# Another order list, pair evictions and four copies moved to GpSimd in an attention-and-maxout kernel

## The chip, the cores and the metric

The kernel runs on one core of one Trainium2 chip. Its time is the device time of one launch in microseconds (us), the median of several runs. A trace of one further execution, taken by the hardware profiler, shows every instruction on the five engines: TensorE (PE, with its weight loads PEld), VectorE (DVE), ScalarE (ACT), GpSimd (POOL) and SyncE (SP, which only issues transfers here).

## What is computed

x has 4 batches of 12544 rows with 128 channels; there are 32 inducing rows; w1 and w2 are 128 x 1024, w_out is 1024 x 128.

```python
def mab(q, kv):
    s = scale * (q @ kv.transpose(0, 2, 1))
    a = softmax(s)
    return a @ kv
h = mab(I, x)                 # 32 rows pool over all of x, per batch
y = mab(x, h)                 # each row of x attends to those 32 rows
h1, h2 = y @ w1, y @ w2
out = np.maximum(h1, h2) @ w_out
```

## The kernel before

The kernel uses max(h1, h2) = h1 + relu(h2 - h1). Both products are linear in h, so for each batch it works out two small matrices: hwd = h (w2 - w1), 32 x 1024, and m1 = h w1 w_out, 32 x 128. With e = exp of the scores of a row against the 32 rows of h, the output row is (relu(e hwd) w_out + e m1), divided by the sum of e.

Per batch there is a pooling part (letters in the order list: x = DMA transposes of x, c = scores and exp, t = DMA transpose of the exponentials, a = accumulation, r = the rest, e, h, w, m = the small matrices) and the main part:

- *stage* (s, L712/L725): scores of a block of up to 16 chunks of 128 rows, four quarters on the four 32-column strips of PE; ACT writes e into an SBUF tile (six of them).
- *phase* (p, L1205): up to four jobs, one per quarter, on the four 32-row strips of PE at once. Each job writes 512 columns of e hwd into one of the eight PSUM banks. In the same stretch the e m1 part of the group that is about to end may run on the fourth strip.
- *eviction of a job* (relu_out, L1107 on DVE, L1110 on ACT): relu from PSUM into an SBUF tile. The number behind the first dot of a phase word is a mask that says which jobs go to DVE. A second number, if given, is a mask of jobs to hold: a held job's eviction waits for the next phase, and if that brings the following job of the same quarter, both banks are evicted in one instruction; any word that isn't a phase lets go of held jobs one by one. The list before has no such second numbers.
- *finals* (plain numbers, L989): so many full 128 x 128 matmuls, relu tile times w_out, added up in one PSUM bank per group of up to four chunks.
- *eviction of a group* (evict_group): multiply by the reciprocal of the sums, on DVE (L1024) or, where the string EVICT has a 1, on ACT (L1031, one instruction per chunk); then SP stores it. There are six output slots.
- *turn_e2* (g, L767 to L780): DMA transpose of e, then halving additions and a reciprocal on POOL. A block without it gets its sums from PE (L819) and DVE (L829).

PE has three kinds of tiling in this kernel: full (finals, transposes, small matrices), row strips (phases) and column strips (stages, pooling). All instructions are issued in the order in which the Python code records them. That order is the string ORDER, one word after another. While recording, the class Clock keeps a rough account of when each engine and bank is free; from that account come the choice of the PSUM bank of each step, the number of filler matmuls (dummies, L619, and keep_busy, L945), and nothing else that is issued.

At the head, w2 - w1 is made on DVE and POOL (difference, L623), H is the step that makes the second half of hwd for batch 0, V transposes w1 on PE (L641) and copies it to SBUF as w1T (L646 DVE, L649 ACT), and W multiplies it with w_out (L662).

small_m1 (L596 to L613) makes m1 on PE and evicts it; for the last batch it also writes the same four 32-row pieces into m1bd, a block-diagonal copy that the last block's full-size matmuls read (linear_full, L963).

The line that assigns an eviction to an engine within a phase:

```python
relu_out(q, blk, [before[1], unit], before[2], ready, vector >> k & 1)
```

## Time and profile before

| | |
|---|---|
| median of 3 runs | 314.69 us (314.38 to 314.78) |
| the profiled execution's own time | 314.68 us |
| its span | 312.9 us |
| granted TensorE clock | 0.998 |
| finals L989, relus | 3104 matmuls |
| relu evictions on ACT (L1110) | 468, mean 620 ns |
| relu evictions on DVE (L1107) | 308, mean 683 ns |
| group evictions on DVE (L1024, 128x512) | 68 and 21 |

The span is what the trace covers, from its first to its last instruction; the execution's time has 1.8 us around it. In rows by group, the columns are: line, engine, operation, what is written and read, shapes and count; then busy us and mean ns of one; then the engine's idle time ahead of such instructions and who ended it. In the chain in order of time a row is: start, us, what ran. In rows of stages: the stretch, its length, then busy us and instructions of each engine, the granted clock, the DMA share, GB/s.

### The profile page before, as it was taken

What the parts mean: (1) busy time and instruction counts of PE and PEld (TensorE: products, weight loads), DVE (VectorE), ACT (ScalarE), POOL (GpSimd) and SP (SyncE); (2) the same over time, 40 slices, a digit from 0 to 9 for tenths busy, and PEclk for the clock granted to TensorE, in tenths of its full rate; (3) what the DMA queues carried; (4) which work ended last, traced back from release to release, by engine and by line L of the source; (5) the groups of instructions that cost most, each with busy time, mean ns of one, the idle gap of its engine ahead of it and who ended that gap; (6) DMA issues with size and microseconds to landing.
All of it is one profiled execution on the core that took longest, in us unless ns stands there. A gap on an engine that the chain in (4) does not pass through costs nothing.

```text
span 312.9 us, 12567 instructions
## 1 busy us (share of the span) xinstructions
PE 306.0 (98%) x5316; PEld 239.4 (77%) x5316; DVE 273.1 (87%) x485; ACT 280.7 (90%) x581; POOL 122.6 (39%) x183
## 2 busy tenths in 40 slices
PE   6999999999999999999999999999999999999996
PEld 2875777777877777778877887778778877788885
DVE  2458999999889999988999998999999899989894
ACT  3668999999989989999999999989999899998875
POOL 7374007910530006677500565139205743288000
PEclk9999999999999999999999999999999999999999
DMA  7999999999399999989699999993422522342223
GB/s 206 208 255 203 218 214 192 167 231 232 107 204 244 256 212 202 212 199 218 136 241 256 185 241 200 194 229 114 131 86 103 153 102 87 118 130 103 103 88 136
DMA packets 80793, 55.69 MB, mean 178 GB/s; under 512 B 62272, under 2 KB 65632, under 8 KB 80736
## 3 DMA queue, kind: packets, MB, share of 16 engines
q1 hardware_dynamic: 74768, 41.19, 56.5%
q0 software_dynamic: 5968, 13.70, 22.6%
q8 instruction: 41, 0.67, 0.9%
q14 instruction: 16, 0.13, 0.1%
HBM read 27.28 MB, written 25.69 MB: 169 GB/s over the span
## 4 chain that ended last, share of the span: by engine, by line
PE 94%; DMA 3%; DVE 1%; issue 1%; POOL 0%; ACT 0%; POOLq 0%
PE psall L989 61%; PE psall L1205 23%; DMA xn<-in_x_dram 3%; PE psall L712 2%; PE psall L458 1%; PE psall L399 1%; PE psall L309 1%; PE psall L371 1%; PE psall L325 1%; DVE relus L1107 1%; PE psall L571 1%; PE psall L504 0%; PE psall L362 0%; DVE hwd L575 0%; PE psall L819 0%
## 5 line engine op out<-in xcount | busy, mean ns | idle before, releaser
L1110 ACT ACTIVATE relus<-psall 128x512 f16<-128x512 f32 x468 | 239.2, 620 | 15.4 <-PE psall L1205 14.4
L1107 DVE TENSOR_SCALAR relus<-psall 128x512 f16<-128x512 f32 x308 | 195.5, 683 | 16.6 <-PE psall L1205 15.7
L989 PE MATMUL psall<-woutp,relus 128*128 128x128 f16 x3104 | 203.7, 220 | 0.0
L989 PEld LDWEIGHTS <-relus 128*128 128x128 f16 x3104 | 174.9, 98 | 33.1 <-issue 27.3
L1205 PE MATMUL psall<-e,hwd 32*128 32x512 f16 (+2 forms) x840 | 81.1, 362 | 0.0
L776 POOL TENSOR_TENSOR half<-ed 128x256 f32<-128x256 f16 (+2 forms) x22 | 13.4, 611 | 145.5 <-DMA ed<-e 145.5
L780 POOL TENSOR_TENSOR rd<-den,minus 128x16 f32<-128x16 f32 (+2 forms) x22 | 57.8, 2628 | 1.7
L1024 DVE TENSOR_TENSOR osbs<-psall,rd 128x512 f32<-128x512 f32 (+1 forms) x80 | 50.9, 637 | 4.3 <-PE psall L1205 1.3
L1205 PEld LDWEIGHTS <-hwd 32*128 32x128 f16 x880 | 27.9, 91 | 11.7 <-issue 2.3
L1205 PE MATMUL psall<-m,e 32*128 32x128 f16 x372 | 36.6, 216 | 0.0
L1205 PEld LDWEIGHTS <-e 32*128 32x128 f16 x372 | 22.2, 92 | 9.6 <-issue 2.0
L776 POOL TENSOR_TENSOR half<-half 128x32 f32<-128x32 f32 (+4 forms) x66 | 21.4, 324 | 5.2
L228 POOL DMA_DIRECT2D xn<-in_x_dram x32 | 17.8, 569 | 5.7 <-DMA xn<-in_x_dram 4.3
L1024 DVE TENSOR_TENSOR osbs<-psall,rp 128x512 f32<-128x512 f32 (+3 forms) x24 | 15.6, 649 | 0.5 <-PE psall L1205 0.4
L313 DVE COPY xT<-psall 128x512 f16<-128x512 f16 (+3 forms) x12 | 5.7, 485 | 8.6 <-PE psall L309 8.4
L413 ACT ACTIVATE eu<-psall 128x512 f16<-128x512 f32 x18 | 10.8, 612 | 0.3 <-PE psall L399 0.2
L725 ACT ACTIVATE e<-psall 128x512 f16<-128x512 f32 (+2 forms) x21 | 10.9, 574 | 0.1
L316 ACT COPY xT<-psall 128x768 f16<-128x768 f16 (+3 forms) x10 | 5.8, 576 | 4.6 <-PE psall L309 4.5
L309 PE MATMUL psall<-identity,xn 128*128 128x128 f16 x98 | 7.5, 219 | 1.5 <-DMA xn<-in_x_dram 1.0
L712 PE MATMUL psall<-xT,hT 128*32 128x512 f16 (+3 forms) x110 | 8.4, 362 | 0.0
L309 PEld LDWEIGHTS <-xn 128*128 128x128 f16 x98 | 5.5, 97 | 3.1 <-DMA xn<-in_x_dram 1.4
L399 PE MATMUL psall<-xT,inducingT 128*32 128x512 f16 x72 | 6.4, 381 | 0.0
(114 smaller groups left out, 129.8 us busy)
## 6 DMA issues: line engine op xcount, KB each, us to landing
out_dram<-osbs SPq DMA_DIRECT2D x90, 256.0 KB, 2.9
xn<-in_x_dram POOLq DMA_DIRECT2D x24, 448.0 KB, 9.9
out_dram<-osbs SPq DMA_DIRECT2D x10, 128.0 KB, 4.3
relus<-in_moe_w_dram POOLq DMA_DIRECT2D x4, 256.0 KB, 5.7
xn<-in_x_dram POOLq DMA_DIRECT2D x4, 224.0 KB, 10.3
xT<-xn SPq DMA_TRANSPOSE x33, 4.3
relus<-in_x_dram SPq DMA_DIRECT2D x1, 512.0 KB, 4.0
relus<-in_x_dram SPq DMA_DIRECT2D x1, 384.0 KB, 4.4
```

Of the source, the lines that this page charges most:

```text
L228: nc.gpsimd.dma_start(out=xn_at[b, i][:, 0:n, :], in_=xr[b, :, k0 : k0 + n, :])
L309: nc.tensor.transpose(ps[:, j, :], xn[:, g + j, :], identity16)
L413: nc.scalar.activation(out=eu, in_=ps, func=AF.Exp, scale=scale, accum_out=st[b]["es"][:, u : u + 1])
L712: nc.tensor.matmul(out=ps[32 * q : 32 * (q + 1), 128 * t : 128 * (t + n)], lhsT=hq, rhs=xT[:, c : c + n, :], start=True, stop=True, tile_p ...
L725: nc.scalar.activation(out=blk.e2[:, 0 : 128 * wd], in_=ps[:, 0 : 128 * wd], func=AF.Exp, scale=st[0]["rs"] if blk.b == 0 else scale,)
L776: nc.gpsimd.tensor_tensor(out=dst, in0=cur[:, :, 0:n], in1=cur[:, :, n : 2 * n], op=ALU.add)
L780: nc.gpsimd.tensor_tensor(out=rp[:, 0:wd, :].rearrange("p t q -> p (t q)"), in0=den[:, 0 : 4 * wd], in1=minus1[:, 0 : 4 * wd], op=ALU.pow,)
L989: nc.tensor.matmul(out=g.ps[lo:hi, 128 * c : 128 * (c + 1)], lhsT=relu[:, lo:hi], rhs=woutp[:, jb, :], start=not g.started, stop=(state["m ...
L1024: nc.vector.tensor_mul(osb[:, 0:m, :], g.ps[:, 0 : m * C].rearrange("p (s c) -> p s c", s=m), g.blk.rp[:, t0 : t0 + m, q : q + 1].broadcas ...
L1107: nc.vector.tensor_scalar(out=dst, in0=src, scalar1=0.0, scalar2=None, op0=ALU.max)
L1110: nc.scalar.activation(out=dst, in_=src, func=AF.Relu)
L1205: nc.tensor.matmul(**seq.pop(0))
```

## The change

Five things change. The constants of Clock: a pair of finals, the switch from row strips to full, the times of two POOL steps. In small_m1 the pieces of m1bd are no longer written by DVE from PSUM but copied by GpSimd from m1. The string ORDER is another list; it also uses hold masks (56 of them), and it puts the transposes x, the turns g, the stages and the finals at other places. EVICT has five ones at other places instead of four, and the last group goes to DVE. The head's order becomes "s p4.12.2 p1.0.1 x1.0 p1.1.1 H1 s V W p2.2 x1.1 p4.8" in place of "s p4.9 s p2.2 H1 V W p2.2 p4.2".

```diff
--- before.py
+++ after.py
@@ -21,11 +21,11 @@
 class Clock:
 
 
-    PAIR = 0.0563
+    PAIR = 0.0559
     COLS = 0.0566
     SWITCH = {
         "full": {"row": 0.095, "col": 0.095},
-        "row": {"full": 0.082, "col": 0.088},
+        "row": {"full": 0.0985, "col": 0.088},
         "col": {"full": 0.1, "row": 0.094},
     }
     STEP = 0.0035
@@ -600,15 +600,17 @@
             end = ck.run(0.06)
             m1 = smp.tile([128, C], F16, name=f"m1_{b}", tag="m1")
             bd = {B - 1: [0, 1, 2, 3]}.get(b, [])
-            outs = [(m1bd[32 * q : 32 * (q + 1), q, :], slice(32 * q, 32 * (q + 1))) for q in bd]
-            for o, r in outs + [(m1, slice(0, 128))]:
-                if b == 0:
-                    nc.vector.tensor_scalar(
-                        out=o, in0=ps[r, 0:128], scalar1=st[0]["rw"][r, :], scalar2=None, op0=ALU.mult
-                    )
-                else:
-                    nc.vector.tensor_copy(out=o, in_=ps[r, 0:128])
-                ck.bank[bi] = ck.on_dve(end, 0.28)
+            if b == 0:
+                nc.vector.tensor_scalar(
+                    out=m1, in0=ps[:, 0:128], scalar1=st[0]["rw"], scalar2=None, op0=ALU.mult
+                )
+            else:
+                nc.vector.tensor_copy(out=m1, in_=ps[:, 0:128])
+            ck.bank[bi] = ck.on_dve(end, 0.28)
+            for q in bd:
+                r = slice(32 * q, 32 * (q + 1))
+                nc.gpsimd.tensor_copy(out=m1bd[r, q, :], in_=m1[r, :])
+                ck.on_pool(ck.bank[bi], 0.3)
             st[b]["m1"] = m1
             st[b]["m1r"] = ck.bank[bi]
 
@@ -630,7 +632,7 @@
                 ck.on_dve(20.4, 0.33)
             else:
                 nc.gpsimd.tensor_copy(out=w1h[:, sl], in_=w1f[:, sl])
-                w_of["cast"] = ck.on_pool(0.0, 0.8)
+                w_of["cast"] = ck.on_pool(0.0, 0.62)
 
         def weights_2():
             turned = []
@@ -885,7 +887,8 @@
         difference(nc.gpsimd, 256, 512, 21.0, 0.64)
         load_x(1, 1)
         load_x(1, 2)
-        difference(nc.gpsimd, 512, J, 22.9, 1.25)
+        ck.pool = 22.98
+        difference(nc.gpsimd, 512, J, 22.9, 1.28)
         cast_w1(1)
         for i in range(3, 7):
             load_x(1, i)
@@ -1227,33 +1230,34 @@
 
         state["stage"] = 1
         ORDER = """
-        s p4.9 s p2.2 H1 V W p2.2 p4.2 14 m0 p3.1 4 p3.2 4 p3.3 15 p4.2 6 x1.0 2 p3.6 15 p4.8 13 p4.5 14
-        p3.1 x1.1 10 p1 p4.6 14 p4.1 20 p4.5 p2.2 16 s x1.2 s p3.5 15 p4.1 g3 18 g4 p3.4 p2.1 x1.3 11
-        x1.4 p4.5 14 p4.1 14 p3.3 10 p4.5 s c1.0 18 p2.1 g5 p3.1 x1.5 x1.6 6 x1.7 6 p4.9 11 x1.8 12 p3.6
-        p3.4 17 s c1.1 p3.4 12 x1.9 3 p4.12 3 x1.10 4 p3.2 11 p4.1 21 p4.2 p2.1 21 p4.6 t1.1 12 p1 p4.5
-        14 c1.2 c1.3 p4.10 23 p3.2 t1.3 p3.2 23 p4.3 18 p2.1 p4.8 28 p4.12 p2 23 g6 p4.5 a1.1 c1.4 a1.3
-        c1.5 p3.4 11 r1 t1.5 14 p4.8 p3.2 31 p2.1 p4.4 9 a1.5 p4.8 5 e1 17 h1 5 p4.3 p3.1 21 w1 6 s s
-        p4.10 25 p3.1 p3.4 33 p4.3 p3.1 24 s s p3.4 18 p2.2 p4.2 11 m1 13 p3.4 4 p4.12 21 p1 p3.2 15 p2.2
-        p4.2 18 p4.5 15 p1.1 p4.2 x2.0 x2.1 14 x2.2 3 p4.5 6 x2.3 13 x2.4 p4.4 p2.1 14 g9 9 x2.5 p3.6 p2
-        13 p4.9 21 p2.2 p4.2 31 x2.6 x2.7 p3.5 p4.1 26 x2.8 g10 c2.0 s p4.12 21 p2.1 p4.8 23 p4.3 10 p3.3
-        c2.1 s c2.2 13 p3.1 7 t2.1 1 p4.3 8 x2.9 2 g11 x2.10 g12 4 p4.3 16 p4.8 13 p4.12 15 p3.2 15 c2.3
-        p3.4 p3.1 28 p3.4 p3.4 22 p4.5 13 s t2.3 c2.4 a2.1 c2.5 p3.1 p3.1 21 g13 7 p2.1 t2.5 p4.2 28 p2.1
-        p4.10 6 r2 22 p3.6 p3 24 p4.1 a2.3 a2.5 p3.2 5 p4.6 14 p4.1 e2 24 p4.3 p3 12 h2 19 p4.1 p2.1 18
-        p4.10 10 p3.4 12 w2 6 p4.14 s s s 23 p2.2 p4.1 24 p3.6 s p3.2 14 p4.8 8 m2 6 p4.4 23 p3.1 p2.2 12
-        g17 2 x3.0 g15 p4.8 21 p2.1 x3.1 x3.2 p4.8 29 p3.1 x3.3 p4.10 24 p3.4 11 p4.9 x3.4 13 p4.4 16
-        p4.10 21 p3.1 p3.2 11 x3.5 x3.6 g1 g16 10 p4.1 x3.7 21 p2.1 p4.1 31 p3.2 p4.3 29 p4.5 10 x3.8
-        p3.5 s s c3.0 c3.1 13 p4.12 18 p3.3 p2 2 t3.1 9 x3.9 x3.10 3 p4.1 18 p3.5 p3 27 p4.9 p2.1 19 s
-        c3.2 c3.3 a3.1 p4.10 p2.1 19 g19 t3.3 g18 p4.9 21 p3.1 p3.1 20 p4.5 r3 21 p3.2 p3.2 31 p4.14 p3
-        27 p4.12 a3.3 c3.4 c3.5 11 p3.3 p3 8 t3.5 23 g20 p4.8 p3.3 31 p2.1 p4.8 23 p4.6 a3.5 p1 p3.4 10
-        p4.1 2 g7 1 e3 10 g14 7 h3 6 p4.3 p3.2 14 w3 3 m3 5 s s s 11 g21 p1 p4.4 21 p4.10 12 p1 p4.6 15
-        p4.8 19 p2.3 p4.2 28 g23 p2.2 p4.2 19 p3.4 3 g22 19 p3.2 p4.6 39 p3.1 p3.2 31 p4.10 p3.2 31 p4.3
-        p2 22 p4.5 11 p3.1 8 p4.1 17 p4.10 14 p3.6 s s s 11 p4.2 8 p3.5 14 g24 p4.1 16 p4.9 12 p4.1 p1.1
-        g8 23 p4.14 p2 15 s p4.1 21 p4.8 p2.1 30 g27 p4.2 p3.5 20 g26 p4.1 18 g25 3 p2.2 p4.1 31 p3.3
-        p4.4 28 p4.12 p1 17 p4.3 18 p2.2 p4.8 31 p3.4 p4.6 1 g2 30 p2.2 p4.8 31 p3.1 p4.5 32 p4.5 p2 30
-        p4.10 p2 24 p4.8 p2.1 32 p3.6 p3.1 23 p2.3 p4.1 36 p2.1 p3.1 24 p4.1 p4.7 56
+        s p4.12.2 p1.0.1 x1.0 p1.1.1 H1 s V W p2.2 x1.1 p4.8 11 m0 4 p3.1.3 4 p3.1 5 p3.5 13 p4.4 11 x1.2
+        p3.4 10 p4.10 13 p4.3 7 x1.3 p3 17 p3.3.1 p2.2.1 11 p4.2 24 p2.1.1 p4.2 22 p3.5 s s 5 p4.10 22
+        p3.5 p2 x1.4 13 p4.6 4 x1.5 10 p4.8.1 g3 13 x1.6 x1.7 g1 p3.5 11 p4.5 c1.0 s 1 x1.8 18 p2.2
+        p3.1.4 11 p4.9 23 p3.5 p3 22 p3.5 x1.9 c1.1 s 11 p4.6 7 p3.2.1 10 p4.1 g4 5 g5 16 p3.5.5 p3.2 21
+        p4.12 10 x1.10 t1.1 p1 p4.6 15 p4.12 c1.2 c1.3 21 p3.3 p3 3 t1.3 19 p4.9 19 p4.15.12 p2 30 p4.1
+        g6 p2.2 22 p4.11 3 c1.4 c1.5 a1.1 a1.3 p3.4 8 r1 t1.5 18 p4.13.15 p3.4 33 p2.2 p4.2 9 a1.5 p4.2 4
+        e1 17 h1 5 p4.10 p3.1 20 w1 6 s s p4.3 24 p3.2.7 p3.2 32 p3.3.2 p4.5 23 s s p3.4 16 p4.1.15 p2.1
+        28 p3.1 p4.1.1 22 m1 p1.1 p3 18 p2.2 p4.1 13 g10 8 p4.12 12 p1 p4.5 8 x2.0 x2.1 5 x2.2 p4.3 21
+        p2.0.1 p4.10 19 x2.3 x2.4 g9 7 p3.2.5 p2.1.1 11 p4.5 x2.5 21 p2.0.2 x2.6 p4.6 x2.7 31 p4.12 p3.2
+        26 s c2.0 p4.6 21 g11 p2.1 p4.2 23 p4.6 10 p3.6 x2.8 c2.1 x2.9 c2.2 s 16 p3.1 3 t2.1 2 x2.10
+        p4.12 14 p4.4 14 p4.3 14 p4.5 g12 14 p3.4 c2.3 15 p2.3.2 p4.2 28 p3.1 p3.4 23 p4.9 t2.3 11 s c2.4
+        a2.1 c2.5 p3.1 p3.4 28 p2.1 t2.5 g13 p4.1 28 p4.4 p2.1 28 r2 2 p3.2 p3.4 24 g8 p4.8 a2.3 a2.5
+        p3.4 5 p4.5 9 e2 4 p4.2 23 h2 4 p4.8 p3.1 31 p4.12.2 p2 21 p4.10 11 p3.1 w2 12 p4.9 s s s 22 p2.2
+        p4.4.1 26 p3.1 s p3.6 14 p4.4 4 m2 14 p4.3 19 p2 p3.6 11 p4.1 g15 2 g16 19 p3.5.1 p3.0.5 x3.0 30
+        x3.1 p3.2 p4.9 x3.2 9 x3.3 12 x3.4 p3.4 10 x3.5 4 p4.10 14 p4.1.1 15 x3.6 p4.12 22 p3.4 p3.1 20
+        p4.2.1 22 p2.2 x3.7 p4.4 31 p4.9.15 x3.8 p3.2 21 g2 6 p4.12 12 p3.5 s s c3.0 x3.9 c3.1 18 p4.5 13
+        t3.1 p3.5 p2.0.1 8 x3.10 3 g17 p4.1 g18 21 p3.6 p3 28 p4.3.15 p2.1 18 s c3.2 a3.1 c3.3 p4.3 p2.1
+        21 p4.12 r3 20 p3.2 p3.2.5 20 p4.2 t3.3 21 p3.6.3 p3.1 30 p4.1.4 p3.5 27 p4.10 a3.3 c3.4 c3.5 11
+        p3.3.1 p3.4.5 6 t3.5 25 p4.2.4 p3.4 7 g19 24 p2.2 p4.4 g14 22 p4.3 a3.5 p1 g20 p3.2 15 e3 p4.2 9
+        h3 16 p3.2 p4.12 13 w3 m3 7 s s s 12 p4.3 g21 11 p1 p4.4 19 g22 p4.3 14 p4.10 p1.0.1 23 p2.1 p4.4
+        28 p2.2 p4.4 21 p3.3 21 p4.9.2 g23 p3.1.4 40 p3.6.7 p3.2 30 p3.4.1 p4.4 30 p4.4 p2.2 21 p4.10 9
+        p3.4 10 p4.8 16 p4.3 11 p3.6 s s s 17 p4.3 g24 9 p3.1 10 p4.1 14 p4.5 14 g25 p4.11.15 p1.0.1 22
+        p2.2 p4.9 15 g26 s p4.12 22 p2.1.1 p4.10 30 p4.5 p3.4 20 p4.12 22 p2.1.1 p4.1 32 p4.10 g27 p3.1.2
+        26 p4.9 16 p1 p4.12 23 p2.1 p4.2 31 p4.10.15 p3.2.7 30 p2.2 p4.8 31 p4.7.2 p3.2.1 31 p4.1 p2.1 28
+        p4.10 p2 24 p4.11.11 p2 30 p3 p3.6 23 p2.2.3 g7 p4.4 32 p2.3.3 p3.2.2 34 p3.6 p3.2.7 52
         """
 
-        EVICT = "000000000000000000000000000000000000000000000000000000000000000000000000000000000000000000000000000000101101"
+        EVICT = "000000000000000000000000000000000000000000000000000000000000000000000000000001000000000000000000000001010110"
 
         WORK = {
             "c": pool_scores,
```

## The prediction

> **What bounds the kernel now.** I read the page first (span, busy shares, the chain that ended last), then the waits, the groups by shape, the chain in order of time at the head, in the middle and at the end, and the busy time by stage. The page and the waits:
>
> ```profile
> span 312.9 us, 12567 instructions
> PE 306.0 (98%) x5316; PEld 239.4 (77%) x5316; DVE 273.1 (87%) x485; ACT 280.7 (90%) x581; POOL 122.6 (39%) x183
> PE 94%; DMA 3%; DVE 1%; issue 1%; POOL 0%; ACT 0%; POOLq 0%
> ...
> DVE relus L1107 <- PE psall L1205: 15.7, 45, 1.1
> ACT relus L1110 <- PE psall L1205: 14.4, 39, 0.9
> ```
>
> TensorE (PE) is the bound: it is busy for 98% of the span and makes up 94% of the chain. ACT and DVE are loaded to 90% and 87% and wait for PE, not the other way round. So the time is the number of matmuls, times their pace, plus the switches between kinds of tiling, plus whatever short waits PE has for a PSUM bank or a relu tile. The pace and the price of a switch come from the chain in order of time (start us, us, what):
>
> ```profile
> 95.58 0.55 PE psall L712 x8
> 96.13 0.33 PE psall L1205 x4
> ...
> 97.57 0.54 PE psall L1205 x6
> ...
> 306.81 1.34 PE psall L989 x24
> ```
>
> 24 final matmuls (L989, 128 columns) take 1.34 us: 0.056 us each. A phase of four 512-column matmuls on four quarters takes 0.33 us where its columns alone are 4 x 0.056 = 0.22: a stretch costs some 0.10 us beyond its columns, the switch. Two phases behind each other take 0.54: one switch for 0.45 us of columns.
>
> The stages (us; then busy us of PE, PEld, DVE, ACT, POOL):
>
> ```profile
> 95.00:107.00 12.00, 12.00 (x201) 8.80 (x199) 11.14 (x22) 11.72 (x25) 0.00 (x0) 1.00 1.07 255
> ...
> 204.00:262.00 58.00, 58.00 (x1015) 46.47 (x1015) 54.06 (x97) 53.30 (x111) 26.24 (x36) 1.00 0.45 130
> 262.00:300.00 38.00, 38.00 (x660) 31.95 (x658) 34.30 (x57) 34.73 (x69) 17.48 (x24) 1.00 0.32 110
> ```
>
> From 95 to 107 us ACT has 0.28 us to spare in 12, later it has 8%. Where the evictions are that dense, a changed order can make PE wait; elsewhere it can hardly win or lose.
>
> **The change part by part.** The constants of the Clock class issue nothing: they act only through the bank that a step chooses and the number of filler matmuls.
>
> *The new order on PE.* I counted both built programs from the first phase (23.06 us in the trace) to the last matmul. Finals (3136), phase matmuls, stagings, pooling matmuls are the same in number and shape. Stretches of one kind of tiling: 347 before, 346 after, so one switch less: -0.10. Row stretches go from 164 to 162; two more phases stand directly behind another one, so two ragged ends of about 0.08 us (the spread of start and end over four quarters) fall away: -0.16. There is one filler matmul more, 0.22 us, ahead of w1T (below): hidden there. Term: **-0.26 us**, bounds -0.4 and 0.
>
> *The head.* The chain there, and the timeline rows beside it:
>
> ```profile
> 23.60 0.02 issue
> 23.63 1.89 DVE relus L1107 x3
> 25.51 0.66 DVE hwd L575
> 26.17 0.34 DVE relus L646
> 26.51 0.05 issue
> 26.56 0.62 PE psall L662 x8
> ...
> 28.15 0.06 PE psall L945
> 28.20 0.02 issue
> ```
> ```profile
> 23.06 0.51 PE L1205 MATMUL psall<-e_first,hwd 32*128 32x256 f16 x9
> ...
> 25.26 0.81 PE L619 MATMUL psall<-warm 128*128 128x512 f16 x3
> ```
>
> PE waits for DVE's copy of w1T, behind three relu evictions and one of hwd. The new order has the same three and one, but the first goes to job 2 of the phase (its last piece is the sixth of nine matmuls) and no longer to job 0, whose last 128-column piece is the ninth. DVE can start about 0.1 us (two 128-column pieces) earlier, at 23.5: L662 at 26.43 and not at 26.56, -0.13. The third filler ends at 26.07 and PE stands still until 26.56; the fourth (0.22) fits into that, and costs 0.22 if the wait should go. Behind it the evictions of p2.2 and p4.8 are queued a little tighter than p2.2 and p4.2 were; from the counts below the first phases lose 0.07 more. Term **-0.06**, bounds -0.2 and +0.3. x1.0 and x1.1 now stand on SP's queue before the first store, and all SP work queues behind them:
>
> ```profile
> 19.65 0.56 POOL L228 DMA_DIRECT2D xn<-in_x_dram  x1
> ...
> 30.35 2.53 SPq L1049 DMA_DIRECT2D out_dram<-osbs  x2
> ```
> ```profile
> xn<-in_x_dram POOLq DMA_DIRECT2D x24, 448.0 KB, 9.9
> ...
> ed<-e SPq DMA_TRANSPOSE x22, 3.1
> ```
>
> Their load is issued at 19.65 and lands by the median of 9.9 at 29.6; the first store is issued at 30.35. Nothing waits: 0, and if the load came a few us late the six output slots still cover it.
>
> *Evictions merged in pairs.* Of 56 hold masks, 29 make a pair: 21 on ACT, 8 on DVE; units per engine hardly move (ACT 473 to 474, DVE 311 to 310). No row shows a two-bank eviction. The nearest rows:
>
> ```profile
> L1110 ACT ACTIVATE relus<-psall 128x512 f16<-128x512 f32 x468 | 239.2, 620 | 15.4 <-PE psall L1205 14.4
> ...
> L1107 DVE TENSOR_SCALAR relus<-psall 128x512 f16<-128x512 f32 x308 | 195.5, 683 | 16.6 <-PE psall L1205 15.7
> ...
> L780 POOL TENSOR_TENSOR rd<-den,minus 128x16 f32<-128x16 f32 x18 | 52.5, 2916 | 1.4
> ...
> L776 POOL TENSOR_TENSOR half<-ed 128x256 f32<-128x256 f16 x18 | 12.0, 666 | 124.3 <-DMA ed<-e 124.3
> ...
> L1031 ACT ACTIVATE osbs<-psall,rd 128x128 f32<-128x128 f32 x10 | 3.1, 383 | 2.0 <-issue 1.0 <-PE psall L963 0.9
> ...
> L337 ACT ACTIVATE et<-psall 128x448 f16<-128x448 f32 x4 | 2.1, 545 | 0.2 <-PE psall L325 0.2
> ...
> L337 ACT ACTIVATE et<-psall 128x224 f16<-128x224 f32 x4 | 1.5, 368 | 0.0
> ...
> L1024 DVE TENSOR_TENSOR osbs<-psall,rd 128x128 f32<-128x128 f32 x4 | 1.2, 288 | 0.4 <-issue 0.2 <-PE psall L1205 0.2
> ```
> ```profile
> 93.91 1.89 DVE L1107 TENSOR_SCALAR relus<-psall 128x512 f16<-128x512 f32 x3 [0.20 <-PE psall L1205]
> 93.99 2.06 ACT L1110 ACTIVATE relus<-psall 128x512 f16<-128x512 f32 x4 [0.47 <-PE psall L1205]
> ```
>
> Four queued ACT evictions take 2.06 us, the last 0.62 of it, so they start 0.48 apart; DVE's 0.60 apart. 224 columns more cost ACT 545 - 368 = 177 ns, so 512 more cost 0.40 and a pair holds ACT for some 0.89 us against 0.96 for two singles: 0.07 less, 1.5 us over 21 pairs. Bounds for a pair: 0.62 (the second bank free) to 1.24 (two full ones). Lighter engines that wait for PE anyway give nothing by themselves; the price is that the first unit's relu and bank come only with the second's. I count both in the next part, with 0.89 and, in the same way (from 288 ns at 128 columns to 683 at 512), 1.13 for DVE.
>
> The Trainium skill, "VectorE: DVE Perf Modes", section "The TRN2 errata — SBUF-src ops pay a fixed extra latency per instruction", gives ScalarE from PSUM a fixed 172 cycles on top of its columns at 1.2 GHz; by it a pair would save 0.14 us (my estimate from that page), 3.0 us over the 21. The trace disagrees with that for queued evictions, since 512 columns 0.48 us apart leave far less than 0.14 to save.
>
> *New short waits.* In both programs I took, for every phase and final, the PE work (at 0.056 a final, 0.22 a 512-column step, 0.10 a switch) between the matmul that releases an eviction and the one that needs its bank or relu, and set against it the evictions queued in between (0.48 and 0.60) and the way there and back. That way is 0.25 from the start of the last matmul to the eviction (309.61 to 309.86 in the last rows of the timeline) and 0.05 behind its end (26.51 to 26.56):
>
> ```profile
> 309.61 0.22 PE L963 MATMUL psall<-m1bd,e 128*128 128x128 f16 x1
> 309.86 0.37 ACT L1031 ACTIVATE osbs<-psall,rd 128x128 f32<-128x128 f32 x1 [0.62 <-PE psall L963]
> ```
>
> One place in full: at 760 finals (about 99 us) the order has p3.1 and p4.1.1 behind each other. The bank that the second phase's last quarter takes was filled by a group whose last final stands 9 finals, a switch and one 512-column step earlier: 0.50 + 0.10 + 0.22 = 0.82 us. Its eviction on DVE needs 0.25 + 0.68 + 0.05 = 0.98. PE waits 0.16. So counted, the new order is short by 0.12 at 462 finals (p4.15.12, six ACT evictions in line), 0.16 at 760, 0.12 at the final behind that, 0.13 at 1870 (p4.3.15), 0.12 at 2562 (p4.11.15), and a few hundredths elsewhere: 0.74 in all. The old order, so counted, is short by 0.18 in all behind 34 us. Term **+0.56**, bounds 0 (they overlap with each other) and +2.3 (a rival).
>
> *Copies of m1 and the rest of GpSimd.*
>
> ```profile
> L963 PE MATMUL psall<-m1bd,e x10: 219/219/219, 306.4 to 309.6; 128*128 128x128 f16 x10
> L610 DVE CAST m1bd<-psall x4: 269/286/297, 231.4 to 232.3; 32x128 f16<-32x128 f32 x4
> ```
>
> DVE loses four casts of 0.286, 1.1 us near 232 us, where the stage leaves it 7% anyhow. POOL gains four copies behind m1. No row has such a copy; if each took as long as POOL's longest operation quoted (2.9), that would be 12 us, and PE reads m1bd first at 306.4. Hidden: 0. The reciprocals: from the order of the DMA turn to the first eviction that reads it the shortest distance is 14.1 us of PE work (15.6 before), against at most 3.1 + 5 x 0.67 + 2.9 = 9.4. Hidden.
>
> *The tail.* The last group's eviction goes from ACT (383 ns) to DVE (288): **-0.09**, bounds -0.15 and +0.1. The store behind it is the same.
>
> Sum: -0.26 - 0.06 + 0.56 - 0.09 = +0.15 us on the profiled execution's 314.68 (span 312.9 and 1.8 around it), which is the median of the runs, 314.69. **Forecast 314.8 us**, no change that can be told: about 0.2% (0.63 us) is what a measurement of this kernel tells from none.
>
> **The rivals.**
>
> *A: the pairs starve PE (slower).* If a two-bank eviction takes near its upper bound, 1.24 and not 0.89, each place above that has a pair in line is later by 0.35 us. It decides where ACT has less than that to spare in a stage: 95 to 107 us has 0.28. Five places x 0.35 = 1.75 on top of the sum: 316.6. For it: 11.72 of 12 us busy, and waits counted there already. Against it: the slope of the two L337 rows.
>
> *B: the lighter engines give the waits back (faster).* If a pair saves 0.14 or more, each counted wait with two or more pairs in line goes, and so do the old order's. Then -0.26 - 0.06 - 0.09 remain, less the old order's 0.18 and the 0.08 of filler and wait at 28.15 (L945): -0.67, 314.0. The page of the Trainium skill named above would have it so. Against it: the largest counted wait (0.16) has no queue ahead of it, just one eviction's length, which no lighter engine shortens.
>
> *C: the list does not do what its words say.* "Dearer switches" should mean fewer of them; it is 346 against 347. So no large gain can be had from there, and this is within the forecast.
>
> **How the numbers follow.** Forecast 0.62, A 0.25, B 0.13. The forecast's own range is 314.1 to 315.5, mostly within 0.2%: it gives 0.53 same, 0.06 slower, 0.03 faster. A is slower (0.25). B gives 0.10 faster, 0.03 same. So faster 0.13, same 0.56, slower 0.31. The range holds the forecast, half of B and the cheaper half of A: 314.0 to 316.4.
>
> **What would show it.** In the profile after: L989's stretches at 0.056 a final, as now; L664 (w1T's matmuls) starting at 26.4; the last eviction on DVE with 0.29 us; two-bank evictions on ACT 0.89 apart when queued; PE waits of 0.1 to 0.2 us near 71, 99, 199 and 261 us and none over 0.3; m1bd's copies done long before 306 us. I am wrong if PE shows a wait over 0.5 us anywhere behind 34 us, if it waits for a DMA turn or a reciprocal, or if w1T comes later than 26.6.

## The result and the profile after

The changed kernel takes **317.48 us** (median of 6 runs, 316.59 to 317.94) against 314.69 (6 runs, 314.38 to 315.25): ratio 1.0085, 95% interval 1.0071 to 1.0099. It is slower, and the time lies above the range 314.0 to 316.4 of the prediction. The profiled execution took 316.59, with a span of 314.8; it is the fastest of the six, so its trace cannot show why the slowest took 1.35 us more.

The page of the changed kernel, and the first lines of its waits:

```profile
span 314.8 us, 12566 instructions
...
PE 306.4 (97%) x5317; PEld 240.2 (76%) x5317; DVE 270.9 (86%) x471; ACT 280.4 (89%) x563; POOL 123.5 (39%) x187
...
PE 94%; DMA 2%; DVE 1%; issue 1%; POOL 0%; ACT 0%; POOLq 0%
```
```profile
DVE relus L1110 <- PE psall L1208: 18.0, 46, 1.1
ACT relus L1113 <- PE psall L1208: 15.5, 41, 1.0
```

By shares nothing has changed: PE is the bound as before, and DVE and ACT even wait longer for it (18.0 for 15.7 us, 15.5 for 14.4). The difference must be looked for in places. I cut each trace at the start of the first phase and at the start of the last matmul (us):

| trace | start to first phase | body | tail, to the end of the span |
|---|---|---|---|
| before | 23.06 | 286.55 | 3.31 |
| after | 23.50 | 286.99 | 4.32 |
| difference | +0.44 | +0.44 | +1.01 |

**Start.** The chain in order of time, before and after:

```profile
16.39 0.39 issue
```
```profile
16.14 0.94 issue
...
26.87 0.62 PE psall L664 x8
```

At 16 us, ahead of all that the change touches, PE waits 0.55 us longer for nothing that the profile shows. A later trace of the kernel with the old list (e9) has 1.17 us there, one of the unchanged changed kernel (e1) starts its first phase at 23.08. So this 0.44 is chance and no part of the change. Counted from the first phase, w1T's matmuls come at 26.87 - 23.50 = 3.37, before at 26.56 - 23.06 = 3.50.

**Tail.** The timeline of the changed kernel at its end:

```profile
306.95 1.89 DVE L1110 TENSOR_SCALAR relus<-psall 128x512 f16<-128x512 f32 x3 [1.01 <-PE psall L1208]
...
308.76 0.68 DVE L1027 TENSOR_TENSOR osbs<-psall,rd 128x512 f32<-128x512 f32 x1
...
309.29 1.58 ACT L1034 ACTIVATE osbs<-psall,rd 128x128 f32<-128x128 f32 x5 [0.72 <-issue]
...
310.75 0.29 DVE L1027 TENSOR_TENSOR osbs<-psall,rd 128x128 f32<-128x128 f32 x1 [1.31 <-PE psall L966]
```

and of the kernel before:

```profile
306.86 1.18 ACT L1031 ACTIVATE osbs<-psall,rd 128x128 f32<-128x128 f32 x4
```

The first of the four last groups used to be evicted by ACT at 306.86, 2.75 us ahead of the last matmul (309.61); now it goes to DVE behind three relu evictions and is evicted from 308.76, 1.7 us ahead of the last matmul (310.49). Its store and the three others now stand closer together: the first of the four is issued 1.03 us ahead of the last matmul and not 1.54. The DMA share and GB/s (last two columns) in the us around and behind the last matmul, before and after, then the time from issue to landing of the last three stores:

```profile
309.60:310.60 1.00, 0.23 (x5) 0.05 (x1) 0.24 (x1) 0.37 (x1) 0.00 (x0) 1.00 0.51 182
```
```profile
310.50:311.50 1.00, 0.21 (x4) 0.04 (x1) 0.29 (x1) 0.38 (x2) 0.00 (x0) 1.00 0.93 342
```
```profile
DMA to landing us min/median/max: 1.6/1.7/1.9
```
```profile
DMA to landing us min/median/max: 1.9/2.5/2.6
```

The last two stores take up to 0.9 us longer to land, and the program ends on them: SP's wait for it, first before, then after (us in total, times, longest):

```profile
SPq L1318 <- DMA out_dram<-osbs: 0.4, 2, 0.3
```
```profile
SPq L1322 <- DMA out_dram<-osbs: 1.3, 2, 1.1
```

That the stores stand closer together is not enough for this. The trace of e6 (below; other evictions ahead, the same end) has the last seven group evictions and the last four stores at the same distances from its last matmul, within 0.01 us, and as full a DMA share in the us behind it; its stores land as fast as those of before, and its tail is 3.44:

```profile
315.14:316.14 1.00, 0.22 (x4) 0.05 (x1) 0.29 (x1) 0.38 (x2) 0.00 (x0) 1.00 0.94 347
```
```profile
DMA to landing us min/median/max: 1.6/1.7/1.9
```

What goes with the long tail is a DMA packet of 8 KB of the kind "instruction". In after it starts 1.42 us behind the last matmul and takes 0.72 us, among the packets of the last two stores. The DMA queues from 1.0 to 2.2 us behind the last matmul, first after, then e6 (queue, kind: packets, MB, share of 16 engines):

```profile
q1 hardware_dynamic: 315, 0.23, 59.3%
q14 instruction: 1, 0.01, 3.8%
```
```profile
q1 hardware_dynamic: 330, 0.24, 62.1%
```

Of the 20 traces of this case, nine have a tail of 3.92 to 4.40, and all nine have such a packet, begun 1.42 to 1.67 us behind the last matmul. The other eleven have tails of 3.28 to 3.75, and in none of them does one begin from 0 to 2.3 us behind it. No run moves this packet alone, so that it is the cause is not shown, nor what puts it there.

**Body.** I set the start of every hundredth final of after (in a repeat, e1) against before. Up to 500 finals the two are within 0.05 us where both stand in finals; between 500 and 600 after loses 0.34. From there the difference stays between 0.38 and 0.70 where both stand in finals; its largest step is one of 0.25 between 1100 and 1200, where a read of xT at 132.71 us starts 0.04 us behind the landing (after's own trace does not have that step). In the stretch from 500 to 600 two matmuls start 0.04 us behind the end of a DVE eviction, so just released; one of them here, in after:

```profile
79.75 0.68 DVE L1027 TENSOR_TENSOR osbs<-psall,rd 128x512 f32<-128x512 f32 x1
...
80.28 0.60 PE L1208 MATMUL psall<-e,hwd 32*128 32x512 f16 x6
```

The group eviction ends at 80.43; of the six matmuls two start at 80.28, the third only at 80.48. It is the kind of wait that was forecast, though at another place. The stage of after that answers to the densest one shown of before:

```profile
95.00:107.00 12.00, 12.00 (x202) 9.24 (x202) 10.59 (x19) 11.81 (x23) 0.00 (x0) 1.00 1.07 244
```

ACT is as full from 95 to 107 us as it was (11.81 for 11.72 us). What this row also shows is the DMA share (the last but one number): above 1, before and after alike. The prediction read it and made nothing of it.

### The profile page after: what moved, and what is told of

Same layout as the page of the kernel before. It is cut to its first block, busy times and chain, and to the rows that moved or that the text cites. A ratio compares the mean times of both kernels' runs of the same rounds, so it can differ in the third digit from the quotient of the medians.

```text
span 314.8 us, 12566 instructions
## 1 busy us (share of the span) xinstructions
PE 306.4 (97%) x5317; PEld 240.2 (76%) x5317; DVE 270.9 (86%) x471; ACT 280.4 (89%) x563; POOL 123.5 (39%) x187
## 4 chain that ended last, share of the span: by engine, by line
PE 94%; DMA 2%; DVE 1%; issue 1%; POOL 0%; ACT 0%; POOLq 0%
PE psall L992 61%; PE psall L1208 23%; DMA xn<-in_x_dram 2%; PE psall L714 2%; PE psall L399 1%; PE psall L458 1%; PE psall L309 1%; PE psall L325 1%; PE psall L371 1%; PE psall L571 1%; DVE relus L1110 1%; PE psall L362 0%; PE psall L504 0%; DVE hwd L575 0%; PE psall L821 0%
## 5 line engine op out<-in xcount | busy, mean ns | idle before, releaser
L1113 ACT ACTIVATE relus<-psall 128x512 f16<-128x512 f32 (+1 forms) x450 | 239.4, 642 | 17.9 <-PE psall L1208 15.5
L1110 DVE TENSOR_SCALAR relus<-psall 128x512 f16<-128x512 f32 (+1 forms) x297 | 193.4, 698 | 19.0 <-PE psall L1208 18.0
L1027 DVE TENSOR_TENSOR osbs<-psall,rd 128x512 f32<-128x512 f32 (+2 forms) x79 | 50.5, 639 | 5.2 <-ACT relus L1113 1.6
L399 PE MATMUL psall<-xT,inducingT 128*32 128x512 f16 x72 | 6.2, 383 | 0.0
```

The lines of the kernel that those rows point to most:

```text
L1027: nc.vector.tensor_mul(osb[:, 0:m, :], g.ps[:, 0 : m * C].rearrange("p (s c) -> p s c", s=m), g.blk.rp[:, t0 : t0 + m, q : q + 1].broadcas ...
L1110: nc.vector.tensor_scalar(out=dst, in0=src, scalar1=0.0, scalar2=None, op0=ALU.max)
L1113: nc.scalar.activation(out=dst, in_=src, func=AF.Relu)
```

## The experiments

All times are medians with ranges; "before" is the kernel before on the same chip, and each ratio is against it (314.92 for e1 to e4). "Profiled" is the traced execution; its three numbers are start to first phase, body and tail, as in the table. A transfer lands when the last of it has arrived; the slack of a read is the time from that landing to the start of the matmul, or weight load, that reads it. In these traces no read starts less than 0.04 us behind its landing, so one that has this slack was waiting. In rows of PE's waits L399 is the pooling's scores (c), L424 its step r, and L458 or L464 its accumulation (a); lines differ a little between kernels. Theory T: the list's end, with that group on DVE and the stores bunched, costs 0.9. Theory D: PE waits for DMA transposes in a part of the runs. Theory B (not the prediction's rival B): other banks, chosen through Clock's account, cost time.

**e1, the changed kernel unchanged.**

> The changed kernel once more, nothing edited, for a second trace. In its first trace (316.59 us, the fastest of six runs) three stretches are longer than before: up to the first phase +0.44, from there to the last matmul +0.47, from the last matmul to the end of the span +0.98. Tail theory: the +0.98 comes back in every execution, since the last groups' evictions and stores are bunched by the list; the median is again 317 to 318. Rival (scatter of the head): the instruction gap at 16 us (0.94 in the changed kernel's trace, 0.39 before) is what differs from run to run; then this trace has another gap there and a tail of about 3.3 us as before.

316.46 (316.06 to 318.32, 6 runs), ratio 1.0061 (1.0038 to 1.0085). Trace: 23.08, body 287.21, tail 4.19. The start is normal again, the long tail is there again. The runs lie 2.3 us apart.

**e2, the changed kernel with the old end** (words of the list and EVICT from group 98 on).

```diff
-  ... p2.2.3 g7 p4.4 32 p2.3.3 p3.2.2 34 p3.6 p3.2.7 52
+  ... p2.3 p4.1 36 p2.1 p3.1 24 p4.1 p4.7 56
-  EVICT ends 01010110
+  EVICT ends 00101101
```

> The changed kernel with the old list's last 18 words and the old EVICT from group 98 on (the last 12 us). Tail theory: the span behind the last matmul falls from 4.3 to 3.3 us and the median by about 1.0, to 316.5. Rival (the waits inside the list): nothing changes beyond 0.2, 317.3.

316.32 (315.3 to 317.2, 10 runs), 1.0043 (1.0028 to 1.0058). Profiled 315.30: 23.07, 287.05, tail **3.40**. In the trace 0.8 of the tail is gone (4.19 in e1). The median meets the expected 316.5 by luck: e1 on the same chip has 316.46, so it fell by 0.14 and not by 1.0, while the runs of both scatter over 2 us. So there is a third thing beside tail and short waits.

**e3, the kernel before with the new end.** The reverse edit.

> The kernel before with the new list's last 19 words and the new EVICT from group 98 on. Tail theory: +1.0, 315.7. Rival (the waits inside the list): no change, 314.6 to 314.9.

316.09 (315.97 to 316.97, 5 runs), 1.004 (1.0024 to 1.0056). Body 287.66, tail 3.45. The median is 1.17 above before, near the number expected, but not by what T says. The finals fall back by 0.86 at 304.4 us, where PE stands for an eviction on ACT:

```profile
304.44 0.37 PE L1205 MATMUL psall<-e,hwd 32*128 32x256 f16 x2 [0.49 <-ACT osbs L1031]
```

Another 0.26 is lost at 139.72 us, far ahead of the edit, where a read of xT has a slack of 0.04 us; in the trace of before that slack is 1.66. So the kernel before, too, can lose time to a late transpose. The tail is only 0.14 longer: the DMA share in the us behind the last matmul is 0.99, yet the stores land within 2.0 us. The new end is dear in both lists, in each in another way; that bunched stores must land late isn't so.

**e4, the kernel before with the new head** (the first 160 words for the first 157).

> The kernel before with the new list's first 160 words (up to 24 groups and a bit, some 90 us), the old list behind. It has the early transposes of x that hold SP's queue for 9.8 us in the trace after (27.4 to 37.2), the new head and the first merged pairs. If the head costs: +0.5 to +1.3, 315.2 to 316.0. Tail theory: +0.1 to +0.3 (the short waits near 34, 72 and 80 us that the trace after shows), 314.8 to 315.0.

315.53 (315.2 to 316.9, 12 runs), 1.0018 (1.0006 to 1.003). The first phases gain (first finals 0.13 earlier, as in after), but in its trace it stands 0.36 behind before at 400 finals and 0.71 at 800. The head alone is no gain in the old list. That doesn't price the head in the changed kernel, whose own trace stands at 0.00 at 400 finals.

The next four ran on another chip (before: 314.92).

**e5, all 33 x words of the changed kernel at the old counts of finals.**

```diff
-  s p4.12.2 p1.0.1 x1.0 p1.1.1 H1 s V W p2.2 x1.1 p4.8 11 m0 4 ...
+  s p4.12.2 p1.0.1 p1.1.1 H1 s V W p2.2 p4.8 11 m0 4 ... 13 p4.4 6 x1.0 ...
```

> The changed kernel with only its 33 x words (DMA transposes of x) put back to the counts of finals at which the old list has them; everything else, the tail too, is the new one. Theory D (the new list lets the pooling's consumers stand right behind the landing of a transpose, so that scattered landings become waits and scatter of the run's time): the waits of L399 near 132.7 and of L424 near 206.1 go, the body is 0.3 to 0.5 us shorter (287.2 to 286.8), the profiled run some 315.9, the median about 316.0 and the scatter half of the unchanged kernel's. Rival (scatter comes from elsewhere, x is hidden): as the unchanged changed kernel within 0.2, 316.3, with the same scatter. Second rival: the old counts put x in front of turns and stores of the new list that need the queue more, then slower, 316.8 and more.

322.17 (322.01 to 322.42, 4 runs), 1.0227 (1.0208 to 1.0246). Far off all that was expected but the second rival. PE waits 1.5 us for one transpose, at the step r of the last batch, which the new list has 39 finals earlier than the old one:

```profile
PE psall L424 <- DMA xT<-xn: 1.5, 1, 1.5
```

But moving x words also moves Clock's account and with it the banks; that the rest of the 6.5 us lost in the body comes from there is argued from e10 (below), not shown. As a test of D it failed.

**e6, without hold masks** (each p word loses its third number).

> The changed kernel without the hold masks: each unit is evicted by itself, engines as the list has them. Theory P (holding a unit until the next phase starves PE at dense places): the short waits behind 72, 80 and 85 us shrink, the body is 0.3 to 0.6 us shorter, profiled 315.8. Rival (the pair lightens ACT by 0.07 us each and that is what keeps the waits short): body 0.3 to 1.0 us longer, profiled 316.6 to 317.3. Neither: within 0.2 of the unchanged changed kernel. If a pair on ACT takes 0.89 between starts the difference per pair is +0.07 us of ACT, if 1.24 it is -0.28.

319.86 (319.54 to 320.35, 5 runs), 1.0151 (1.0131 to 1.017). The body is 292.24. It tests less than I meant, for a merged unit takes the engine of the later phase; without masks 12 units move from ACT to DVE, and the banks differ:

```profile
L1113 ACT ACTIVATE relus<-psall 128x512 f16<-128x512 f32 x459 | 235.8, 621 | 25.7 <-PE psall L1208 23.9 <-ACT relus L1113 1.0
...
L1110 DVE TENSOR_SCALAR relus<-psall 128x512 f16<-128x512 f32 x317 | 201.0, 684 | 16.9 <-PE psall L1208 15.6
```

The price of a pair itself stands in after's rows:

```profile
L1113 ACT ACTIVATE relus<-psall 128x1024 f16<-128x1024 f32 x21 | 21.7, 1036 | 1.0 <-PE psall L1208 1.0
...
L1110 DVE TENSOR_SCALAR relus<-psall 128x1024 f16<-128x1024 f32 x8 | 9.7, 1216 | 0.4 <-PE psall L1208 0.4
```
```profile
80.95 1.94 ACT L1113 ACTIVATE relus<-psall 128x1024 f16<-128x1024 f32 x2 [0.99 <-PE psall L1208]
```

Two queued pairs take 1.94, the last 1.04 of it: 0.90 apart, forecast 0.89. Rival A (1.24) is out. By this row a pair saves 0.06 against two singles (2 x 0.48), not the 0.14 that the prediction estimated from the Trainium skill, "VectorE: DVE Perf Modes", section "The TRN2 errata — SBUF-src ops pay a fixed extra latency per instruction".

**e7, the pieces of m1bd on DVE again.**

> The changed kernel with the pieces of m1bd written by DVE from PSUM again, as before. My step (the copies on GpSimd are hidden and DVE has room near 232 us): no change within 0.2 us of the unchanged changed kernel. Rival (DVE is short near 232 and the move is a gain): 0.2 to 1.1 us longer. Rival (the copies on GpSimd hold up reciprocals behind them): shorter by 0.2 or more.

318.71 (317.91 to 319.96, 6 runs), 1.012 (1.0099 to 1.0142). The edit is at 2175 finals, and the program ahead of it is the same, yet 1.25 us against e1 are lost between 1000 and 1200 finals: PE waits for xT at 125 and 134 us. That is D, unasked. A further 1.9 follows behind 1900 finals, part of it waits behind evictions (0.5 and 0.2 us): counted in the built programs, 86 matmuls follow another matmul in their bank than in the changed kernel. So e7 does not price the copies by its time. The copies on GpSimd themselves are short and lie where nothing waits for them:

```profile
L612 POOL COPY m1bd<-m x4: 284/288/296, 232.1 to 233.1; 32x128 f16<-32x128 f16 x4
```

**e8, e5 with the old end.**

> The changed kernel with the old counts for the x words, and from group 98 on the old list and the old assignment of group evictions. Theories D and T (the tail's last group on DVE bunches the last stores, 0.9 us) add up: tail 3.4 us, body 286.7 to 286.9, profiled 315.0 and a median of 315.1 to 315.4, with a scatter like that of the kernel before. If D fails: as the changed kernel with the old tail alone, 315.3 profiled and 316.3 median.

321.85 (320.73 to 322.31, 5 runs), 1.0208 (1.0187 to 1.0229): as e5, and as a test it failed for the same reason. Its tail is 4.09 with the old end, and it has the instruction packet, 1.67 us behind the last matmul.

The next four, on one chip (before: 314.63), separate account and issue.

**e9, the kernel before with the two new constants of Clock; e10, the changed kernel with the two old ones.**

```diff
-    PAIR = 0.0563
+    PAIR = 0.0559
-        "row": {"full": 0.082, "col": 0.088},
+        "row": {"full": 0.0985, "col": 0.088},
```

> The kernel before with only the two changed constants of Clock (PAIR 0.0559, the switch from row strips to full 0.0985); list, evictions and copies as before. These issue no instruction; they change the bank that a step chooses. My prediction gave them nothing by themselves. Theory B (a list fits the banks that came with it; other banks make PE wait at many dense places): slower than before by 0.5 to 3 us, spread over the whole body. Rival (banks hardly matter): within 0.3 us of before, 314.9.

> The changed kernel with the two constants of before (PAIR 0.0563, switch 0.082); list, evictions and copies new. Theory B: slower than the unchanged changed kernel of this call by 0.5 to 3 us, in the body. Rival (banks hardly matter): within 0.3 us of it.

e9: 314.69 (314.38 to 316.12, 12 runs), 1.0001 (0.9988 to 1.0015); its finals are within 0.02 us of before's all the way (taken from the first phase on). e10: 321.16 (319.81 to 321.46, 5 runs), 1.0192 (1.017 to 1.0215), 4.3 above the control e12; PE waits at new places:

```profile
PE psall L1208 <- ACT osbs L1034: 0.8, 1, 0.8
PE psall L1208 <- ACT relus L1113: 0.5, 1, 0.5
PE psall L399 <- DMA xT<-xn: 0.3, 1, 0.3
```

Most of the old list's changed banks are only a renaming: counted in the built programs, 3393 of 5312 matmuls write another bank in e9, but only 28 follow another matmul in their bank than before. Between the changed kernel and e10 it is 2469 and 196 of 5313. Theory B holds for the new list and not for the old. Constants that issue nothing are worth 4 us to one list and nothing to the other. From here on the account stays where it was, and only the issue of a transfer is moved.

**e11, ten transposes issued 11 to 80 finals earlier, the account unmoved** (an X word issues, the x word only counts).

```diff
-  x2.6 p4.6 x2.7 31 p4.12 p3.2 26 s c2.0 ... p3.6 x2.8 c2.1 x2.9 c2.2
+  x2.6 p4.6 x2.7 X2.7 31 p4.12 p3.2 X2.8 26 s c2.0 p4.6 X2.9 ... p3.6 x2.8 c2.1 x2.9 c2.2
```

> The changed kernel with ten DMA transposes of x (x2.5 to x2.10, x3.7 to x3.10) issued 11 to 80 finals earlier, their account in Clock left where it was, so that every bank and every PE instruction is the same as in the unchanged changed kernel. Theory D (landings of these transposes come so near to their consumers that a part of the runs waits): the waits of L399 near 125 and 133 us and of L424 near 206 go, the scatter of the runs falls to that of before (about 0.5 us), the median to 0.3 to 1.5 us below the control of this call. Rival (the DMA engines are full there, earlier issue lands nothing earlier, or pushes stores and turns back): no gain, or up to 1 us slower, with waits at other transposes.

> The unchanged changed kernel again, as a control for this call: 316.3 to 318.7. If this chip is one on which the transposes land later, its waits of L399 and L424 are longer than the 0.2 to 0.3 us of the first repeat, and the median is 317.5 or more; if the list alone sets them, 316.4.

e12, the control: 316.84 (315.55 to 317.67, 6 runs), 1.0064 (1.0041 to 1.0087). Its trace is the best evidence of D. Against e1, the same program, every hundredth final is within 0.02 us up to 1000; then 0.61 and 0.72 are lost at two pooling steps, and behind that it stays at 1.29 to 1.33 up to the last final. Its waits from 118 to 142 us and the rows of its timeline:

```profile
PE psall L399 <- DMA xT<-xn: 0.9, 2, 0.7
```
```profile
125.43 0.39 PE L399 MATMUL psall<-xT,inducingT 128*32 128x512 f16 x2 [0.21 <-DMA xT<-xn]
...
133.94 0.39 PE L399 MATMUL psall<-xT,inducingT 128*32 128x512 f16 x2 [0.67 <-DMA xT<-xn]
```

e11: 320.72 (318.59 to 323.39, 6 runs; 320.49 without the slowest), 1.0205 (1.0165 to 1.0246). The waits for xT are gone as D had it, but the gain isn't there; PE waits for the transposes of the exponentials instead, which now stand behind them, first from 118 to 142 us, then from 200 to 209:

```profile
PE psall L464 <- DMA eT<-eu: 1.3, 1, 1.3
```
```profile
PE psall L464 <- DMA eT<-eu: 0.9, 1, 0.9
```

So here the earlier transposes of x delayed those of the exponentials, as the rival had it; the loss is larger than it said.

**e13, two transposes only: x2.8 at 982 finals and not 1036, x2.9 behind t2.1; e14, the same with the old end; e15, the reverse in the kernel before; e17, control** (before: 314.92).

> The changed kernel with two transposes at the old list's places: x2.8 issued at 982 finals and not at 1036, x2.9 behind t2.1 and not ahead of it; their account in Clock stays where it was, so PE's instructions and all banks are those of the changed kernel. Theory D1 (their places make c2.3 wait): the wait of L399 near 133 us goes, eT_2_1 is no later; the median is 0.4 to 1.2 us below the control's, the scatter smaller. Rival D2 (the DMA engines are full there and any order makes something wait): the wait moves to another transpose, no gain beyond 0.3 us.

> The same two transposes, and from group 98 on the old list and old assignment of group evictions. If tail (0.9) and these landings are what is left beside the waits behind evictions (0.4 to 0.5 us): profiled 315.1 to 315.4, median 315.2 to 315.6, which is 1.2 to 1.8 us below the control. Rival D2: the tail's gain alone, 0.7 to 0.9 below the control.

> The kernel before with x2.8 and x2.9 issued at 1035 finals, ahead of t2.1, as in the new list; account, PE's instructions and banks as before. Theory D1: c2.3 (at 1129 finals, where the new list has it at 1113) waits in a part of the runs: median 0.1 to 0.6 us above before and a wider scatter. Rival D2 (or c2.3's place decides): as before within 0.2 us.

> The unchanged changed kernel as the control on this chip: 316.3 to 317.5; waits for xT0 near 125 and 133 us between 0 and 1.3 us in the trace.

e13: 316.15 (315.46 to 317.46, 7 runs), 1.0043 (1.0027 to 1.0059). e17: 316.72 (315.75 to 317.39, 6 runs), 1.0057 (1.004 to 1.0074). The difference of 0.57 has the sign of D1, but the ranges overlap, and e13's own trace waits at 125.45 and 139.92, so the wait near 133 us has only moved, as D2 said. e15: 314.73 (314.45 to 316.21, 12 runs), 1.0001 (0.999 to 1.0012): the late places alone cost the old list nothing, against D1. e14: 315.89 (315.06 to 317.19, 9 runs), 1.0036 (1.0021 to 1.0051); its trace is one without such waits up to 200 us: 22.96, body 286.94, tail 3.39, 315.06 in all. Its sum closes: 315.06 - 314.68 is body +0.39, tail +0.08 and start -0.10. But the median is above the 315.2 to 315.6 expected; it is 0.83 below e17's, which is what D2 gave (0.7 to 0.9). In e17 the waits are in the last batch (200 to 209 us):

```profile
PE psall L458 <- DMA eT<-eu: 0.4, 1, 0.4
PE psall L424 <- DMA xT<-xn: 0.3, 1, 0.3
```

**e18, e13 with the turn g10 at 982 finals and not 813; e19, the kernel before with g10 at 813 and not 981** (before: 314.73). SP's timeline shows what led to them, first before, then e12:

```profile
103.39 2.86 SPq L1049 DMA_DIRECT2D out_dram<-osbs  x2
106.34 4.30 SPq L241 DMA_TRANSPOSE xT<-xn  x3
```
```profile
103.59 0.33 SPq L1052 DMA_DIRECT2D out_dram<-osbs  x1
104.03 1.45 SPq L769 DMA_TRANSPOSE ed<-e  x1
106.23 0.33 SPq L1052 DMA_DIRECT2D out_dram<-osbs  x1
106.66 6.07 SPq L241 DMA_TRANSPOSE xT<-xn  x3
```

In the new list the turn of block 10 is issued at 104 us, while two of seven loads of 448 KB, issued from 85 us on, are still under way (they land at 105.4 and 108.0). It takes 8.0 us to land, where the turns from 112 to 140 us have a median of 2.6, and the transposes behind it are late:

```profile
DMA to landing us min/median/max: 8.0/8.0/8.0
```
```profile
ed<-e SPq DMA_TRANSPOSE x3, 2.6
```

> The changed kernel with three transposes at the old list's places: the turn g10 at 982 finals and not at 813, x2.8 at 982 and x2.9 behind t2.1; accounts in Clock left where they were, PE's instructions and banks those of the changed kernel. Theory D3 (g10 falls into the loads and makes the transposes behind it late): x2.0 lands 1.5 to 2 us earlier (111 and not 112.8), the waits for xT0 near 125, 133 and 140 us are gone, slack there 0.4 or more, and the body up to 1200 finals is that of the first repeat or shorter; the median 0.3 to 0.8 us below 316.15 (the same without g10), what is left being the tail and batch 3's transposes near 203 and 207 us. Rival D2 (the engines are full, the order does not matter): as the run without g10, 316.15, within 0.2 us.

> The kernel before with the turn g10 issued at 813 finals and not at 981, where the new list has it; PE's instructions and banks as before. Theory D3: x2.0 lands 1.5 to 2 us later (112.5), c2.2 waits for xT0 near 125 us in the trace or has less than 0.2 us of slack (before 0.4), and the median is 0.2 to 0.8 us above before. Rival D2: within 0.2 us of before, slack as before.

The landing of x2.0 behind its issue, before, e12, e18 and e19:

```profile
DMA to landing us min/median/max: 4.3/4.3/4.3
```
```profile
DMA to landing us min/median/max: 6.2/6.2/6.2
```
```profile
DMA to landing us min/median/max: 4.8/4.8/4.8
```
```profile
DMA to landing us min/median/max: 5.6/5.6/5.6
```

e19: 315.03 (314.86 to 316.52, 12 runs), 1.0009 (0.9992 to 1.0026). Its trace does what D3 said: x2.0 lands at 111.9 and not 110.6, the slack of 0.44 us at c2.2 becomes a wait, and between 1000 and 1300 finals 0.33 us are lost that stay to the end. The median's +0.30 agrees, though its interval holds 1. e18's trace does it the other way at first: x2.0 lands at 111.6, slack at 125 us is 1.38 (e12: none). But a read of xT at 139.30 now has a slack of 0.04 us, and the finals fall back by 0.33 there, which is about what was won against e1 (0.3); profiled 316.49. Its runs, 317.99 (316.0 to 319.69, 8 runs), 1.009 (1.006 to 1.0121), are 1.1 to 1.3 slower than the controls e12 and e17 on other chips. So g10 is shown to take away the slack at c2.2; that putting it back mends the kernel is not, and the wait only moved, as in e13.

## Why the prediction was wrong, point by point

The seven traces of the new list with its own end and banks have a tail of 4.07 to 4.40; seven with the old end have 3.28 to 3.40. But an eighth with the old end, e8, has 4.09, and five with the new end and other banks, evictions or list ahead of it (e3, e5, e6, e7, e10) have 3.44 to 3.92: the end's words alone don't decide it. The body is 286.94 where transposes cost less than 0.1 us in all (e14), and up to 288.53 where they come late. So after is 0.4 (short waits) + 0.8 to 1.1 (tail) + 0 to 1.6 (transposes) above before: 315.9 to 317.8 from 314.7, which holds the median of all four sets of runs of it (317.48, 316.46, 316.84, 316.72). Two things don't fit: the fastest untraced runs of it, 315.55 (e12) and 315.75 (e17), lie below that, and the old end lowered the median by 0.14 (e2 against e1) and 0.26 (e14 against e13) only, where the traces have 0.8 and 0.9.

- *Head, PE order and new short waits, +0.24 together*: the body, in which all three lie, showed +0.39 where no transpose was late. The sum was near and the places were not: around the forecast places at 760 and 1870 finals the difference moves by 0.06 at most, and most of it arises between 500 and 600.
- *The head by itself, -0.06*: w1T -0.13 as forecast, +0.04 by 500 finals. "Nothing waits" for x1.0 and x1.1 was wrong in its reason: x1.1 held SP's queue for 9.8 us, and the first store went out at 37.21 and not at 30.35:

```profile
25.85 11.31 SPq L241 DMA_TRANSPOSE xT<-xn  x2
37.21 1.15 SPq L1052 DMA_DIRECT2D out_dram<-osbs  x2
```

  The cover that the prediction named, six output slots, took it with 3.7 us to spare at 45 us in after's trace and 1.1 to 1.5 in its repeats (before: 7.1).
- *Pairs*: 0.90 for 0.89 on ACT; on DVE 1.22 long. Rival A falls with it, and B with the 0.06 saved.
- *Copies of m1*: 288 ns each, done at 233 us, hidden.
- *The tail, -0.09*: **this step failed first.** It followed one eviction, the last, which did become shorter (0.29 for 0.37), and said that the store behind it is the same. That store was not the same: it took 2.5 us to land and not 1.6, and the tail grew by 0.8 to 1.1. The prediction didn't ask what else moves in that us. The group that EVICT moved behind three relu evictions, and the stores that so stand closer together, cost 0.1 by e3 and e6; the rest goes with an 8 KB instruction packet in all nine long tails, which is not shown to be the cause.
- *The transposes*: **here a term was missing.** I followed the changed places of x and g to the stores and the reciprocals, but not to the matmuls that read xT and eT, though the prediction quoted a stage with a DMA share of 1.07 and listed a wait over 0.5 us, or for a DMA turn, as signs of being wrong. e12 has such a wait: 0.67 us for an xT. Before, a weight load of eT already has no slack (0.04 us at 76.76), and the smallest slack of an xT is 0.44 (124.69). In the four traces of the changed kernel reads near 125, 133, 203 and 206 to 207 us start 0.04 to 0.06 us behind a landing, in each trace others of them. 0 to 1.6 us, different from run to run.
- *Clock's constants*: they do nothing in the old list, as forecast; but the new list takes 4.3 us more without them, so the two could not be priced one by one.

What stays open: whether the instruction packet makes the tail long, and what puts it there; why e18's runs are slow though its trace loses only 0.33 us to a landing; and what makes landings differ from run to run. On the last, the traces show one thing more. A 16 KB instruction packet starts at 107 to 110 us in all 20 of them. Where it takes 0.9 us, x2.0 lands 4.2 to 4.9 us behind its issue; where it takes 1.2, 5.4 to 5.6; where it takes 1.6 to 2.2, 5.8 to 6.5. Which of the two delays the other, or whether a third thing delays both, no run shows. None of the kernels tried is measurably faster than before; the best trace of the new list, e14, is 0.4 us above it.

## What to carry to other kernels

When a list moves transfers, follow each one to the instruction that reads it, and note its slack in the trace before: where the DMA share is near 1, a slack of a few tenths can be spent by one transfer put ahead (0.44 us in e19), and here the loss showed as scatter of the runs first. At the end of a kernel follow all last stores and whatever else the DMA engines carry beside them, instructions too, not the last eviction alone. And when an account decides hidden things like banks, keep it fixed in an experiment and move the issue only, or the experiment measures the account.

## What the runs showed of the hardware

- A transpose issued on SP while loads ran held the queue: 9.8 us for the second of the two in the 25.85 row, though the load that it reads had landed at 25.84. Issued at 104 us into loads from GpSimd's queue, one took 6.2 to 8.0 us to land in the traces of the changed kernel where its like have a median of 2.6 to 2.8 behind the loads. The Trainium skill, "DMA: Bandwidth & Descriptors", section "Issuing engines are not separate DMA queues", says that transfers of all issuing engines run on the same 16 engines and interleave; these rows agree.
- The same program on the same data lost 0 to 1.6 us in its body to landings, by traces of four executions that are within 0.02 us of each other up to 1000 finals.
- Instructions come by DMA as well: an 8 KB packet of them, 0.5 to 0.8 us long, lay among the last stores in all nine traces whose tail is 3.92 to 4.40, and in none of the eleven with shorter ones.
- Two-bank evictions: ACT 1036 ns long and 0.90 apart when queued (one bank 620 and 0.48), so merging saves 0.06 us; DVE 1216 ns long (one bank 683), and as no eviction stands queued right behind one of its eight, what merging saves there is not shown.
